# Spreading POOL's additions of y over four slots in an attention and GELU kernel

## The chip, the cores and the metric

The kernel runs on one core of one Trainium2 chip. The metric is the device time of one execution in microseconds; the kernel before takes 1471.4 us (median of three runs, 1471.25 to 1472.25). The core's engines work side by side, each through its own instructions in order: TensorE (PE in the profile; PEld is its loading of weights) multiplies matrices into PSUM, VectorE is DVE, ScalarE is ACT, GpSimd is POOL, and SyncE (SP) issues DMAs here.

## The reference

```python
# attention: q, k, v are (8, 8, 576, 64), float32
scores = scale * np.matmul(q, k.transpose(0, 1, 3, 2))
kth = np.partition(scores, -top_k, axis=-1)[..., -top_k:-top_k + 1]   # top_k = 32
scores = np.where(scores >= kth, scores, -1000000000.0)
attn = np.exp(scores - np.max(scores, axis=-1, keepdims=True))
attn = attn / (np.sum(attn, axis=-1, keepdims=True) + 1e-09)
x = np.matmul(attn, v)            # then (B, H, S, D) -> (4608, 512)
# mlp: w_in is (512, 2048), w_out is (2048, 512)
h = x @ w_in
g = 0.5 * h * (1.0 + erf(h * inv_sqrt2))
out = g @ w_out
```

Each row of scores keeps only its 32 largest entries; then a softmax, the product with v, and a two-layer network with an exact GELU.

## The kernel before

**Slots.** The attention is cut into 144 items, each a tile of 128 query rows for a pair of heads. The main loop runs over slots n = 0 to 147, and every slot issues one step of several items at once: scores of items n+2 and n+3 (PE, then ACT), the search for the 32nd largest score of item n (DVE, `top_k`), selection and softmax of item n-1 (ACT, lines 538 and 550), transposition of item n-2, the product with v of item n-3 (PE, `attend`, tile o, line 736 or 747). All engines take the instructions in the order in which the loop writes them; there is no planner, and an engine runs ahead of the others as far as its data and buffers allow.

**The top-k.** DVE halves the work by keeping, of every two scores, the larger in one list (`larger`, line 443) and the smaller in another. POOL makes the second list: `sum_up` (line 468) adds the two as integers, `smaller` (line 476) subtracts the larger. DVE then alternates maxima of eight (line 504) with replacements (line 507).

**POOL's slot.** Once the top-k of item n has ended, POOL computes the threshold (lines 518 and 519), multiplies item n-1 by the inverse of its sum (`normalise`, line 573), and sums the lists of item n+2 (line 468). Behind that stands what the change touches, `run_small`. The next slot brings `smaller` (476) and the small addition to the softmax's sum (line 531, `add_small`), for whose result DVE waits with its reciprocal (line 525) at the end of its top-k. ACT's selection of the next slot waits for the threshold.

**Transposing by DMA.** From the middle of the run on, half of the items go through HBM: DVE transposes blocks (line 599), SP writes the tile (`write_p`, line 609, tensor turned) and reads it back in the next slot (`read_p`, line 619, tile pt), which PE then uses as weights of o.

**The network.** As soon as the rows of x for a block of tokens are there, its products go into the slots in pieces: even slots take the first layer (tile h_ps, line 805), odd ones the second layer. A block has 256 tokens, or 128 at the end of the sequences. For 256 tokens the second layer is computed with seven products in place of eight (tiles seven and y_ps, lines 959 and 961). For that POOL forms four sums of each group of gelus (`sums`, lines 842 to 845), right behind the gelus, and adds the products up afterwards.

**The additions.** These go to a list, `small`, as pairs of a size and a function. In each of the second to fourth odd slots of a block one addition of the seventh product is put at its head (line 982; ACT has copied that product to tile p in line 980). The last slot of a block adds seven more: lines 1010 to 1014, then `lower` (line 1021) and `upper` (line 1025). The last two also register the store of 128 finished rows, which SP issues one slot later (line 876). `run_small(room)` first runs the sums that are due, each for 4 of its room, and then takes from the list while room is left:

```python
        while summing:
            sums(summing.pop(0))
            room -= 4
        while small and room > 0:
            n, f = small.pop(0)
            f()
            room -= n
```

A block of 128 tokens needs no sums and ends with one entry of size 2 (lines 936 and 937). Tiles y, part and y7 have two buffers each. `few[0]` is true from slot 13 on, when PSUM is shared more sparingly. Past slot 144 the pieces that are left run one after the other, and `run_small(9)` is called from elsewhere.

Of the kernel before, what the change touches and what calls it, by code (L numbers as in the profile page):

```python
# [14 lines left out]
def kernel(  # L15
# [261 lines left out]
    few = [False]  # L277
# [552 lines left out]
    def sums(u):  # L830

        g = g_of[u].rearrange("p x (f n) -> p x f n", f=2)
        a11, a21, a12, a22 = (g[:, :, f, h * P : (h + 1) * P] for f in range(2) for h in range(2))
        if u == NU - 2:
            t = work.tile([P, 2 * S], f32, tag="s", bufs=7, name="sum_s")
            t = t[:, 0 : 6 * P].rearrange("p (x k n) -> p x k n", x=2, k=3)
            add = nc.vector.tensor_tensor
        else:
            t = work.tile([P, 2, 3, P], f32, tag="sum", bufs=1, name="sum")
            add = nc.gpsimd.tensor_tensor  # L840
        s1, s2, s4 = (t[:, :, x] for x in range(3))
        add(s1, a21, a22, op=ALU.add)
        add(s2, s1, a11, op=ALU.subtract)
        add(a21, a11, a21, op=ALU.subtract)
        add(s4, a12, s2, op=ALU.subtract)
        sums_of[u] = t

    def weight_sums(j):

        e, o = w_out_sb[:, 2 * j], w_out_sb[:, 2 * j + 1]  # L850
        t2, t3, t4 = (w_sum[:, j, x] for x in range(3))
        nc.gpsimd.tensor_tensor(t3, o[:, B2], e[:, B2], op=ALU.subtract)
        nc.gpsimd.tensor_tensor(e[:, B2], e[:, B2], e[:, B1], op=ALU.subtract)
        nc.gpsimd.tensor_tensor(t2, o[:, B2], e[:, B2], op=ALU.subtract)
        nc.gpsimd.tensor_tensor(t4, t2, o[:, B1], op=ALU.subtract)
        summed.add(j)

    summing, summed = [], set()
# [107 lines left out]
    seven, small = [None], []  # L966
# [121 lines left out]
    def run_small(room):  # L1088
# [8 lines that stand above are left out]
# [93 lines left out]
    for n in range(ahead):  # L1190
# [149 lines left out]
        sum_up(n + 2)  # L1340
        if n in sums_in:
            weight_sums(sums_in[n])
        run_small(6)

        if n > 0 and not waits(unit_in(n + 1)):
            weights_size(unit_in(n + 1))
# [52 lines left out]
```

## Time and profile before

| | |
|---|---|
| median of the runs | 1471.4 us (1471.25 to 1472.25) |
| profiled execution | 1471.37 us |
| its span, first to last instruction | 1469.6 us |
| PE, DVE, POOL, ACT busy | 99%, 89%, 77%, 73% |
| POOL, one addition of 128 x 256 | 0.73 us |
| POOL, normalise (line 573) | 2.12 us |
| POOL, lines 468 and 476 | 1.43 and 1.41 us |

The profile is of one execution. In rows of the timeline stand start, duration, engine, line, operation, the tile written and the tiles read, and in brackets how long the engine had been idle and what it waited for. A row of waits reads "engine, tile and line that waited, what released it: us in total, times, longest". In the chain a row has the start, the time and the engine with its tile and line. Ends of matmuls are modelled: each is shown longer than the distance to the next.

### The profile page before, as it was taken

Reading aid. Unit: us, or ns where it says so; the run is one execution under the profiler, and the core shown is the slowest. Engines: PE = TensorE matmul, PEld = TensorE weight load, DVE = VectorE, ACT = ScalarE, POOL = GpSimd, SP = SyncE. Lnnn points to the kernel's source line nnn. Section 1 sums busy time; section 2 is a strip of 40 time slices with the busy share of each in tenths; the row PEclk is TensorE's granted clock in tenths of the full one; section 3 lists DMA queues with packets and bytes.
Section 4 is the critical chain, followed back from the end, with each engine's and each line's share of the span. In section 5 each row is a group of like instructions: output and inputs, shape, how many; then the busy total and the mean of one; then the engine's idle time right before and its main releaser. Section 6 shows DMA issues by size and latency. Waiting matters only on the chain. (4 is left out here: it accounts for less than half of the span.)

```text
span 1469.6 us, 26630 instructions
## 1 busy us (share of the span) xinstructions
PE 1450.9 (99%) x8720; PEld 1135.9 (77%) x8720; DVE 1312.0 (89%) x3328; ACT 1069.3 (73%) x1905; POOL 1138.1 (77%) x1290
## 2 busy tenths in 40 slices
PE   8999999999999999999999999999999999999999
PEld 6776677877777777887777778787777777787887
DVE  7999899999999899999999999999989989999701
ACT  7999977777777786767777777776777767687620
POOL 6877667878798879877798978887888887987632
PEclk9999999999999999999999999999999999999999
DMA  7524210045435246345534345444543423633200
GB/s 196 147 87 127 82 48 1 24 92 109 79 76 96 56 84 134 65 102 107 106 75 83 71 71 119 87 92 95 104 96 75 89 48 81 128 66 74 62 15 15
DMA packets 527050, 123.51 MB, mean 84 GB/s; under 512 B 452256, under 2 KB 518464, under 8 KB 526912
## 3 DMA queue, kind: packets, MB, share of 16 engines
q1 hardware_dynamic: 525648, 121.39, 38.7%
q8 instruction: 69, 1.13, 0.3%
q14 instruction: 69, 0.57, 0.1%
q10 hardware_dynamic: 1200, 0.39, 0.1%
q0 software_dynamic: 64, 0.03, 0.0%
HBM read 78.70 MB, written 43.06 MB: 83 GB/s over the span
## 5 line engine op out<-in xcount | busy, mean ns | idle before, releaser
L805 PE MATMUL h_ps<-xT,w_in_sb 128*128 128x256 f32 (+1 forms) x2560 | 534.1, 361 | 0.0
L805 PEld LDWEIGHTS h_ps<-xT,w_in_sb 128*128 128x128 f32 x2560 | 437.5, 190 | 73.3 <-issue 12.9
L504 DVE MAX8 top<-lists 128x8 f32<-128x576 f32 (+1 forms) x792 | 475.3, 639 | 0.0
L507 DVE MATCH_REPLACE8 lists<-top,lists 128x288 f32<-128x288 f32 (+1 forms) x528 | 307.4, 587 | 0.0
L538 ACT ACTIVATE s<-s,stat 128x576 f32<-128x576 f32 x288 | 217.6, 778 | 100.9 <-POOL stat L518 100.9
L573 POOL TENSOR_TENSOR s<-s,stat 128x1152 f32<-128x1152 f32 x135 | 285.9, 2118 | 0.3 <-DVE stat L525 0.3
L550 ACT ACTIVATE s<-s,stat 128x576 f32<-128x576 f32 x288 | 223.7, 780 | 7.3
L468 POOL TENSOR_TENSOR lists<-s 128x576 int32<-128x576 int32 x133 | 189.8, 1427 | 0.0
L476 POOL TENSOR_TENSOR lists<-lists 128x576 int32<-128x576 int32 x132 | 186.1, 1410 | 4.0
L531 POOL TENSOR_SCALAR stat<-stat 128x2 f32<-128x2 f32 x144 | 31.4, 218 | 166.6 <-ACT s L550 160.3
L736 PE MATMUL o<-pt,raw_v 128*64 128x256 f32 x1280 | 152.9, 384 | 3.2 <-DMA pt<-turned 2.0
L416 ACT ACTIVATE s<-s_ps 128x1024 f32<-128x1024 f32 x127 | 124.9, 1030 | 42.1 <-PE s_ps L408 42.0
L736 PEld LDWEIGHTS o<-pt,raw_v 128*64 128x64 f32 x1280 | 87.5, 136 | 87.5 <-issue 42.2
L961 PE MATMUL y_ps<-w_out_sb,sum 128*128 128x256 f32 x472 | 140.4, 379 | 0.0
L408 PE MATMUL s_ps<-kt,qm 64*128 64x512 f32 x512 | 129.6, 619 | 0.8 <-ACT s L414 0.8
L821 ACT ACTIVATE g<-h_ps 128x512 f32<-128x512 f32 x144 | 78.2, 595 | 71.1 <-PE h_ps L805 70.5
L961 PE MATMUL y_ps<-w_out_sb,g 128*128 128x256 f32 x480 | 114.2, 380 | 0.0
L507 DVE MATCH_REPLACE8 lists<-first,lists 128x288 f32<-128x288 f32 x264 | 114.1, 437 | 0.0
L443 DVE TENSOR_TENSOR lists<-s 128x576 f32<-128x576 f32 x133 | 108.6, 817 | 4.3 <-ACT s L381 2.2
L504 DVE MAX8 first<-lists 128x8 f32<-128x288 f32 x268 | 106.3, 435 | 0.0
L680 ACT COPY pt<-tp 128x1024 f32<-128x1024 f32 x76 | 77.6, 1021 | 37.4 <-PE tp L665 37.3
L961 PEld LDWEIGHTS y_ps<-w_out_sb,g 128*128 128x128 f32 x480 | 91.0, 190 | 12.4
(162 smaller groups left out, 2406.9 us busy)
## 6 DMA issues: line engine op xcount, KB each, us to landing
turned<-s SPq DMA_DIRECT2D x228, 144.0 KB, 3.6
pt<-turned SPq DMA_DIRECT2D x228, 144.0 KB, 3.1
raw_v<-in_v_dram SPq DMA_DIRECT2D x64, 128.0 KB, 2.6
raw_q<-in_q_dram SPq DMA_DIRECT2D x112, 72.0 KB, 2.4
raw_k<-in_k_dram SPq DMA_DIRECT2D x112, 72.0 KB, 2.4
out_dram<-y SPq DMA_DIRECT2D x30, 256.0 KB, 2.2
w_out_sb<-in_moe_w_in_dram SPq DMA_DIRECT2D x14, 511.8 KB, 4.9
w_out_sb<-in_moe_w_out_dram SPq DMA_DIRECT2D x10, 511.8 KB, 4.1
```

The source lines that it names most:

```text
L408: nc.tensor.matmul(s_ps[:, e], lhsT=q_t[rows, :], rhs=kt[rows, main_keys(pair)], start=True, stop=True)
L416: nc.scalar.activation(spread(s, S + TL, SM), s_ps, func=AF.Copy, scale=scale)
L468: nc.gpsimd.tensor_tensor(t[:, :, 1].bitcast(i32), a.bitcast(i32), b.bitcast(i32), op=ALU.add)
L476: nc.gpsimd.tensor_tensor(into_of(i)[:, :, 1].bitcast(i32), both, top, op=ALU.subtract)
L504: nc.vector.max(x[:, e], src[:, e])
L507: nc.vector.match_replace(dst[:, e], x[:, e], src[:, e], LOWEST)
L538: nc.scalar.activation(s, s, func=AF.Prelu, bias=st["neg"][:, e : e + 1], scale=1.0, alpha=STEEP)
L550: nc.scalar.activation(s, s, func=AF.Exp, bias=st["bias"][:, e : e + 1], scale=1.0, accum_out=st["den"][:, e : e + 1],)
L573: nc.gpsimd.tensor_tensor(s, s, wide, op=ALU.mult)
L736: nc.tensor.matmul(o[e * D : (e + 1) * D, 0:n], lhsT=vt[:, j, e, :], rhs=pt[:, e * NJ + j if j < NM else NM, :], start=(j == 0), stop=(j = ...
L805: nc.tensor.matmul(h_tile(u)[:, i, :], lhsT=w_in_sb[:, ko, f * P : (f + 1) * P], rhs=xT[:, ko, c0 : c0 + n], start=(ko == 0), stop=(ko == ...
L961: nc.tensor.matmul(acc[names][:, k], lhsT=lhsT, rhs=rhs, start=(j == 0 and k == 0), stop=(j == FT // 2 - 1 and k == 1),)
```

## The change

The room given to `run_small` at the end of a slot becomes dependent on what the slot holds. From slot 13 on, a slot with sums gets 5 in place of 6, so one entry of the list follows the sums. A slot without sums gets the length of the list less three, at least three.

```diff
@@ -1340,7 +1340,7 @@
         sum_up(n + 2)
         if n in sums_in:
             weight_sums(sums_in[n])
-        run_small(6)
+        run_small(6 if not few[0] else 5 if summing else max(3, len(small) - 3))
 
         if n > 0 and not waits(unit_in(n + 1)):
             weights_size(unit_in(n + 1))
```

## The prediction

> **What bounds the kernel now.** I read the page's busy rows first, then the chain for the rate of TensorE, then what each engine waited for, then the stretch of one batch of additions in order of time.
>
> ```profile
> PE 1450.9 (99%) x8720; PEld 1135.9 (77%) x8720; DVE 1312.0 (89%) x3328; ACT 1069.3 (73%) x1905; POOL 1138.1 (77%) x1290
> ```
> ```profile
> 1293.69 1.92 PE s_ps L408 x8
> 1408.13 6.91 PE h_ps L805 x32
> ```
> ```profile
> L805 PEld LDWEIGHTS h_ps<-xT,w_in_sb 128*128 128x128 f32 x2560 | 437.5, 190 | 73.3 <-issue 12.9 <-ACT s L538 12.3 <-ACT g L821 0.5
> ```
>
> TensorE is busy for 99% of the span. A busy PE need not be at its peak, so the rate decides: 32 matmuls took 6.91 us, 216 ns each, and the load of one weight tile takes 190 of these. Back to back there is nothing between them to win. A gain must therefore come out of moments when PE stood still. Behind the start-up and ahead of the tail (130 to 1360 us) these are all the waits of PE, and below them those of DVE:
>
> ```profile
> PE o L736 <- DMA pt<-turned: 2.0, 2, 1.2
> PE tp_t L373 <- ACT p L980: 1.2, 3, 0.4
> PE o L747 <- ACT p L980: 0.8, 3, 0.3
> PE o L736 <- issue: 0.4, 1, 0.4
> ```
> ```profile
> DVE stat L525 <- POOL stat L531: 65.1, 65, 2.9
> DVE lists L443 <- ACT s L381: 2.2, 4, 0.7
> ```
>
> So PE lost some 4.4 us in 1230, while DVE stood 65 us waiting for POOL's L531. DVE's lateness is absorbed by buffers, nearly always. The question is whether the few waits of PE come from the slots with six additions. These are the six that are not of o L747, and the matmuls ahead of the last:
>
> ```profile
> 424.81 0.49 PE L373 MATMUL tp_t<-kt,qm 128*128 128x128 f32 x2 [0.41 <-ACT p L980]
> 584.95 0.62 PE L736 MATMUL o<-pt,raw_v 128*64 128x256 f32 x3 [0.37 <-issue]
> 770.26 0.49 PE L373 MATMUL tp_t<-kt,qm 128*128 128x128 f32 x2 [0.42 <-ACT p L980]
> 931.23 0.65 PE L736 MATMUL o<-pt,raw_v 128*64 128x256 f32 x4 [1.23 <-DMA pt<-turned]
> 1116.25 0.49 PE L373 MATMUL tp_t<-kt,qm 128*128 128x128 f32 x2 [0.40 <-ACT p L980]
> 1274.01 1.99 PE L408 MATMUL s_ps<-kt,qm 64*128 64x512 f32 x8
> 1276.73 0.62 PE L736 MATMUL o<-pt,raw_v 128*64 128x256 f32 x3 [0.73 <-DMA pt<-turned]
> ```
>
> By the code's count of slots, six additions stand together in slots 40, 48, 56, 76, 84, 92, 112, 120 and 128; the tp_t waits are in slots 43, 79 and 115, those of o in 60, 96 and 132, each three or four slots behind one. 584.95, 931.23 and 1276.73 are one ring of two batches apart (346.28 and 345.50), so I count the first, whose releaser the row calls issue, with the other two.
>
> **The change, part by part.** Call m the slot in which the last products of 256 tokens end. They leave eight additions (L982, L1010 to L1014, L1021, L1025). In nine of thirteen places the next gelus are summed in slots m and m+2. There the old rule does sums + 2, then 6, sums, nothing. The new one does sums + 1; then 7 are left and max(3, 7 - 3) = 4 run; then sums + 1; then 2. In the other four places (the next block has 128 tokens, no sums in m) 6 + 2 becomes 5 + 3. At the end of the program nothing differs, since run_small has another caller there. No instruction is added or removed. One place of the nine, POOL in order of time:
>
> ```profile
> 743.71 0.73 POOL L1010 TENSOR_TENSOR y<-y 128x256 f32<-128x256 f32 x1
> 744.39 1.41 POOL L476 TENSOR_TENSOR lists<-lists 128x576 int32<-128x576 int32 x1
> 750.42 0.72 POOL L1011 TENSOR_TENSOR y<-y,y 128x256 f32<-128x256 f32 x1
> 752.60 0.74 POOL L1014 TENSOR_TENSOR y<-y,y 128x256 f32<-128x256 f32 x1
> 753.28 0.74 POOL L1021 TENSOR_TENSOR y<-y,y 128x256 f32<-128x256 f32 x1
> 754.66 1.42 POOL L476 TENSOR_TENSOR lists<-lists 128x576 int32<-128x576 int32 x1
> 756.16 0.22 POOL L531 TENSOR_SCALAR stat<-stat 128x2 f32<-128x2 f32 x1
> 765.05 0.22 POOL L531 TENSOR_SCALAR stat<-stat 128x2 f32<-128x2 f32 x1
> 765.85 0.22 POOL L518 TENSOR_SCALAR stat<-top 128x2 f32<-128x2 f32 x1 [0.58 <-DVE stat L525]
> 770.20 1.40 POOL L476 TENSOR_TENSOR lists<-lists 128x576 int32<-128x576 int32 x1
> 773.23 0.22 POOL L531 TENSOR_SCALAR stat<-stat 128x2 f32<-128x2 f32 x1 [1.63 <-ACT s L550]
> ```
> ```profile
> 756.41 0.17 DVE L525 RECIPROCAL stat<-stat 128x2 f32<-128x2 f32 x1 [2.18 <-POOL stat L531]
> 756.49 0.76 DVE L443 TENSOR_TENSOR lists<-s 128x576 f32<-128x576 f32 x1
> ```
>
> Slot m: L1010 goes, and L476 and L531 come 744.39 - 743.71 = 0.68 us sooner. Slot m+1: L1014, L1021 and L1025 go (752.60 to 754.66, 2.06 us) and L1010 comes in (0.68), which saves 1.38 more. L531 falls from 756.16 to 754.10, and DVE, ready since 756.41 - 2.18 = 754.23 and that too up to 0.68 sooner, goes on 2.06 us earlier. Slot m+2: L1014 costs POOL 0.68, so its L531 comes 2.06 - 0.68 = 1.38 sooner; the threshold L518 waited there for DVE (0.58) and so comes between 1.38 and 2.06 sooner. ScalarE's selection hangs on that threshold, its gelus and the copy of p (L980) on the selection, and tp_t on that copy: 1.38 us covers a wait of 0.42. Slot m+3: two additions cost 754.66 - 753.28 = 1.38 us, between L468 and L476, and lie in POOL's idle time ahead of L531, 1.63 here. What hides them is that L531 waits for the softmax (L550) anyway; without that cover they cost DVE 1.38 us at each place. The smallest idle of that slot among the nine, and that of the last:
>
> ```profile
> 427.78 0.22 POOL L531 TENSOR_SCALAR stat<-stat 128x2 f32<-128x2 f32 x1 [1.61 <-ACT s L550]
> 1275.06 0.22 POOL L531 TENSOR_SCALAR stat<-stat 128x2 f32<-128x2 f32 x1 [1.97 <-ACT s L550]
> ```
>
> So I take nothing for them, with 12.4 us of DVE time (nine times 1.38) as the far end.
>
> The stores move too. L1021 and L1025 register them, and SP issues them in the slot behind: m+4 in place of m+2, the parity is kept. On SP this is what stands there in the third place of each ring:
>
> ```profile
> 1261.06 2.58 SPq L619 DMA_DIRECT2D pt<-turned  x4
> 1263.73 1.02 SPq L876 DMA_DIRECT2D out_dram<-y  x2
> 1264.85 4.00 SPq L609 DMA_DIRECT2D turned<-s  x4
> 1271.57 2.54 SPq L619 DMA_DIRECT2D pt<-turned  x4
> 1280.67 3.35 SPq L609 DMA_DIRECT2D turned<-s  x4
> ```
> ```profile
> 1261.80 1.36 DVE L599 STREAM_TRANSPOSE s<-s 128x1152 f32<-128x1152 f32 x1
> ```
>
> The data of the write at 1264.85 was there at 1263.16 (1261.80 + 1.36), and SP had been at the stores since 1263.73. Without them the write starts at about 1263.74, 1.1 us sooner, and so do the read behind it and PE's o, late by 0.73. In the new place the stores fall between 1274.11 and 1280.67, where SP has 6.5 us with nothing to issue: cost 0. What could be late next are the buffers: y, part and y7 have two each, and their next user in the nine places is ScalarE at slot m+8, behind the store of m+4; in the four others the additions end in m+1 as before.
>
> Sum: the waits of pt give 2.0 + 0.4, but of the 1.23 only the 1.1, so 2.3; those of tp_t 1.2. The idle time shown begins at the modelled end of a matmul; s_ps really hands on after 1.92 us and not 1.99 (0.07 three times). For tp_t the modelled 379 ns against 216 add 0.16 three times. Together 2.3 + 1.2 + 0.2 + 0.5 = 4.2 us. The three of o L747 (0.8) I leave in:
>
> ```profile
> 1263.83 0.27 ACT L757 COPY xT<-o 128x128 f32<-128x128 f32 x1 [2.19 <-PE o L747]
> ```
>
> ScalarE itself waits there for PE, so POOL is not their cause. The profiled execution took 1471.37 us (span 1469.6, 1.8 around it), the median of the runs is 1471.4: the forecast is 1471.4 - 4.2 = 1467.2. Whatever stays off PE's path comes to nothing, since the matmuls keep their 216 ns.
>
> **The rivals.** *DVE loses it again.* DVE's L443 reads two halves of s. Mostly it takes 0.76, but where it began late, beside POOL's normalisation, it took 2.61:
>
> ```profile
> 1339.36 2.61 DVE L443 TENSOR_TENSOR lists<-s 128x576 f32<-128x576 f32 x1 [0.46 <-ACT s L381]
> ```
>
> A DVE that is 2 us ahead meets s unfinished more often, and each meeting costs 2.61 - 0.76 = 1.85 of the 2.06. The tp_t waits would stay, and the store's share come: 1471.4 - 2.5 = 1468.9, not told from no change. Against it: only four waits on L381 in all now. The Trainium skill, SBUF — State Buffer, section SBUF: two separate sides, says that GpSimd and a VectorE instruction with two SBUF inputs take a shared port as an exclusive lock, the loser blocked for the whole instruction. By that rule this meeting is no accident; the 2.61 agrees with it.
>
> *The reads are not SP's.* If the waits for pt hang on how fast the DMAs land, only tp_t's 1.7 comes: 1469.7. For it speaks that the four writes took 4.00 us at 1264.85 and 3.35 at 1280.67, though the stores just ahead may be why.
>
> *Slower: the cover in slot m+3 is gone.* ScalarE's softmax ends sooner than POOL's two additions; it decides as soon as the 1.61 falls under 1.38. Then L531, DVE and the next threshold are late in a slot that had no such load, and each of nine places gains a tp_t wait of 0.58 while the old ones stay: 1471.4 + 5.2 = 1476.6. Against it: both sides of that idle time start from the same threshold, so shifting it leaves the 0.23 us of margin.
>
> *PE was not the bound.* Then DVE's 2.06 at nine places comes in full: 1471.4 - 18.5 = 1452.9. The Trainium skill, Perfetto Trace Analysis, section Identifying the Most-Contended Engine, says that matmul busy time misleads and that the share of weight loads is to be read. By that rule PE has 23% free here (77%), which would speak for this rival. The rows speak against it: 190 of 216 ns is 88% where nothing stands still.
>
> **How the numbers follow.** About 0.2%, 2.9 us, is what a measurement of this kernel tells from no change. Forecast (1465.0 to 1468.4): 0.60. DVE loses it again 0.13, reads not SP's 0.12: these two lie within 0.2%. Slower 0.11. PE not the bound 0.04. Faster: 0.60 less 0.02 for its upper edge, and 0.04, is 0.62; same 0.27; slower 0.11. The range takes in the forecast's own, whose low end has the L747 waits (0.8 and 0.5 of pipelining) and a little more gone, and both small rivals up to no change: 1465.0 to 1471.6; outside are the slower case and the large gain, 0.15.
>
> **What would show it.** POOL's timeline has 4, 1 and 2 additions in m+1, m+2, m+3. DVE's wait for L531 falls from 65 us by up to 18; L531's idle in m+3 falls from 1.6 to about 0.2. The waits of PE for pt and of tp_t for p are gone, and the stores stand behind a read with nothing on their heels. The forecast is wrong if PE's waits reappear behind m+3, if L443 takes over 2 us in new places, or if POOL's later L476 lets DVE wait in the middle of a top-k.

## The result, and the profile after

The changed kernel takes 1467.4 us in the median of nine runs (1467.1 to 1467.9), the kernel before beside it on the same chip 1471.6 (1470.9 to 1473.6): a ratio of 0.9971, with a 95% interval of 0.9961 to 0.9981. The forecast was 1467.2 us, within 1465.0 to 1471.6. The profiled execution took 1467.42 us, 3.95 less than the one of before, with a span of 1465.7.

The row of busy times of the changed kernel, which answers to the first row shown in the prediction:

```profile
PE 1449.4 (99%) x8720; PEld 1134.9 (77%) x8720; DVE 1313.4 (90%) x3328; ACT 1070.1 (73%) x1905; POOL 1137.9 (78%) x1290
```

The instructions are as many as before on every engine, and PE is still busy for 99%. The difference has to lie in the moments when PE stood still. All its waits between 130 and 1360 us in the changed kernel, then those of DVE (us in total, times, longest):

```profile
PE o L747 <- ACT p L980: 0.8, 3, 0.3
PE tp_t L373 <- ACT p L980: 0.5, 2, 0.3
```
```profile
DVE stat L525 <- POOL stat L531: 58.7, 70, 3.4
DVE lists L443 <- ACT s L381: 3.1, 5, 0.7
```

PE's waits for pt (2.4 us with the one put down to issue) are gone, and those of tp_t fell from 1.2 to 0.5. The total went from 4.4 to 1.3 us. That tp_t waits for a copy of another product comes from the code: from slot 13 on, tp_t (here the scores of the last keys, line 373), seven and o take turns in one PSUM buffer (`bank`, tag z). A tp_t behind seven can start only when ScalarE has copied that product out (L980, or L977 for the first of a block).

The place that the prediction showed, in the changed kernel, POOL in order of time:

```profile
742.65 1.42 POOL L476 TENSOR_TENSOR lists<-lists 128x576 int32<-128x576 int32 x1
...
748.69 0.73 POOL L1010 TENSOR_TENSOR y<-y 128x256 f32<-128x256 f32 x1
749.49 0.73 POOL L1011 TENSOR_TENSOR y<-y,y 128x256 f32<-128x256 f32 x1
...
751.56 1.41 POOL L476 TENSOR_TENSOR lists<-lists 128x576 int32<-128x576 int32 x1
...
760.47 0.74 POOL L1014 TENSOR_TENSOR y<-y,y 128x256 f32<-128x256 f32 x1
...
762.66 0.22 POOL L531 TENSOR_SCALAR stat<-stat 128x2 f32<-128x2 f32 x1
762.95 0.22 POOL L518 TENSOR_SCALAR stat<-top 128x2 f32<-128x2 f32 x1
...
767.88 0.73 POOL L1025 TENSOR_TENSOR y<-y,part 128x256 f32<-128x256 f32 x1
...
770.34 0.22 POOL L531 TENSOR_SCALAR stat<-stat 128x2 f32<-128x2 f32 x1 [0.36 <-ACT s L550]
```

The rows left out are marked by dots. Four additions (L1010 to L1013) stand in slot m+1, one (L1014) in m+2, two (L1021, L1025) in m+3. To see what that moved, the two kernels need a common clock. DVE's reciprocal ahead of this place, untouched by it, was at 735.75 before and at 734.67 after, so the changed kernel came into the place 1.08 us ahead. DVE in the kernel before, and then in the changed one:

```profile
735.75 0.14 DVE L525 RECIPROCAL stat<-stat 128x2 f32<-128x2 f32 x1
```
```profile
734.67 0.14 DVE L525 RECIPROCAL stat<-stat 128x2 f32<-128x2 f32 x1
...
753.31 0.17 DVE L525 RECIPROCAL stat<-stat 128x2 f32<-128x2 f32 x1 [0.81 <-POOL stat L531]
```

From there on, each step against the rows of the prediction, less 1.08: L476 behind slot m 0.66 us sooner (744.39 to 742.65), DVE's reciprocal behind slot m+1 2.02 sooner (756.41 to 753.31), L531 behind m+2 1.31 sooner (765.05 to 762.66), the threshold L518 there 1.82 sooner (765.85 to 762.95), L531 behind m+3 1.81 sooner (773.23 to 770.34). The idle time ahead of this last one fell from 1.63 to 0.36.

Where the 3.95 us arose is seen from the start of the same matmul in both traces: both kernels issue the same 8720 matmuls in the same order. This is by how much the changed kernel gained on the kernel before around each place, in us, worked out from the two traces:

```
at (us, before)   gained                 the matmul
 425, 770, 1116   +0.67  +0.69  +0.66    tp_t L373
 585, 931, 1277   +0.26  +1.30  +0.80    o L736, reading pt
 579, 924, 1270   +0.17  +0.15  +0.16    small steps up to tp_t L651
 598, 944, 1290   -0.08  -0.52  -0.53    tp_t L373
1388              +0.15                  the tail
```

The tp_t matmuls give 2.02, those of pt 2.36, the small steps 0.48 and the end 0.15; 1.13 go back. The rest of 0.1 is in hundredths. What goes back is new waits of tp_t some 13 us behind each pt place. PE in the changed kernel, at a place where it had no wait before:

```profile
941.42 0.49 PE L373 MATMUL tp_t<-kt,qm 128*128 128x128 f32 x2 [0.26 <-ACT p L980]
```

SP at the third place of the ring, in the changed kernel (the rows that answer to those of the prediction), and below it PE's matmuls, the last of which read that pt:

```profile
1256.42 3.09 SPq L619 DMA_DIRECT2D pt<-turned  x4
1259.62 3.46 SPq L609 DMA_DIRECT2D turned<-s  x4
1265.78 3.56 SPq L619 DMA_DIRECT2D pt<-turned  x4
1269.38 1.07 SPq L876 DMA_DIRECT2D out_dram<-y  x2
1277.13 3.36 SPq L609 DMA_DIRECT2D turned<-s  x4
```
```profile
1270.47 1.99 PE L408 MATMUL s_ps<-kt,qm 64*128 64x512 f32 x8
1272.39 2.38 PE L736 MATMUL o<-pt,raw_v 128*64 128x256 f32 x20
```

The write follows the read at once, and the stores stand behind the next read with 6.68 us free after them (1270.45 to 1277.13). PE goes from s_ps to o without a gap.

### The profile page after: what moved, and what is told of

Same layout as the page of the kernel before. It is cut to its first block, busy times and chain, and to the rows that moved or that the text cites. A ratio compares the mean times of both kernels' runs of the same rounds, so it can differ in the third digit from the quotient of the medians.

```text
span 1465.7 us, 26622 instructions
## 1 busy us (share of the span) xinstructions
PE 1449.4 (99%) x8720; PEld 1134.9 (77%) x8720; DVE 1313.4 (90%) x3328; ACT 1070.1 (73%) x1905; POOL 1137.9 (78%) x1290
## 3 DMA queue, kind: packets, MB, share of 16 engines
q8 instruction: 69, 1.13, 0.3%
## 5 line engine op out<-in xcount | busy, mean ns | idle before, releaser
L573 POOL TENSOR_TENSOR s<-s,stat 128x1152 f32<-128x1152 f32 x135 | 286.4, 2121 | 0.3 <-DVE stat L525 0.3
L550 ACT ACTIVATE s<-s,stat 128x576 f32<-128x576 f32 x288 | 224.1, 781 | 7.5 <-issue 0.4
L476 POOL TENSOR_TENSOR lists<-lists 128x576 int32<-128x576 int32 x132 | 186.2, 1411 | 3.3
L531 POOL TENSOR_SCALAR stat<-stat 128x2 f32<-128x2 f32 x144 | 31.4, 218 | 167.2 <-ACT s L550 155.8
L736 PE MATMUL o<-pt,raw_v 128*64 128x256 f32 x1280 | 152.9, 384 | 0.9 <-ACT pt L670 0.4
L736 PEld LDWEIGHTS o<-pt,raw_v 128*64 128x64 f32 x1280 | 86.9, 136 | 85.7 <-issue 42.6
L821 ACT ACTIVATE g<-h_ps 128x512 f32<-128x512 f32 x144 | 78.2, 594 | 75.7 <-PE h_ps L805 75.2
L443 DVE TENSOR_TENSOR lists<-s 128x576 f32<-128x576 f32 x133 | 109.9, 827 | 5.1 <-ACT s L381 3.1
L680 ACT COPY pt<-tp 128x1024 f32<-128x1024 f32 x76 | 77.6, 1020 | 39.9 <-PE tp L665 39.7
```

The lines of the kernel that those rows point to most:

```text
L476: nc.gpsimd.tensor_tensor(into_of(i)[:, :, 1].bitcast(i32), both, top, op=ALU.subtract)
L550: nc.scalar.activation(s, s, func=AF.Exp, bias=st["bias"][:, e : e + 1], scale=1.0, accum_out=st["den"][:, e : e + 1],)
L573: nc.gpsimd.tensor_tensor(s, s, wide, op=ALU.mult)
L736: nc.tensor.matmul(o[e * D : (e + 1) * D, 0:n], lhsT=vt[:, j, e, :], rhs=pt[:, e * NJ + j if j < NM else NM, :], start=(j == 0), stop=(j = ...
```

## The experiments

The change does two things at once: it moves stores by two slots, and it spreads additions. The table gives each kernel by the additions that it has in slots m, m+1, m+2 and m+3 of the nine places. "Late" stores stand where the changed kernel has them, "early" ones where the kernel before has them. Kernel before in the four calls: 1471.6, 1471.3, 1471.5 and 1471.7 us.

| kernel | additions | stores | us | ratio to before (95%) |
|---|---|---|---|---|
| before | 2, 6, 0, 0 | early | 1471.6 | 1 |
| changed | 1, 4, 1, 2 | late | 1467.4 | 0.9971 (0.9961 to 0.9981) |
| stores_late | 2, 6, 0, 0 | late | 1470.4 | 0.9991 (0.9982 to 0.9999) |
| dummy_stores | 1, 4, 1, 2 | late, and dummies early | 1469.4 | 0.9989 (0.9980 to 0.9998) |
| eight_in_one | 0, 8, 0, 0 | early | 1474.4 | 1.0017 (1.0008 to 1.0026) |
| four_four | 4, 4, 0, 0 | early | 1480.4 | 1.0058 (1.0045 to 1.0070) |
| one_in_m | 1, 7, 0, 0 | late | 1471.5 | 0.9998 (0.9989 to 1.0007) |
| two_in_m | 2, 4, 0, 2 | late | 1467.6 | 0.9973 (0.9962 to 0.9983) |
| four_last | 1, 3, 0, 4 | late | 1467.6 | 0.9969 (0.9956 to 0.9981) |
| six_later | 1, 0, 0, 7 | late | 1472.7 | 1.0007 (0.9998 to 1.0016) |
| no_seven | 1, 0, 0, 0 | late | 1467.3 | 0.9967 (0.9955 to 0.9980) |
| p_first | 1, 4, 1, 2 | late | 1493.1 | 1.0144 (1.0131 to 1.0158) |

### The stores alone: stores_late

The additions stay as before. The stores go through one more list and are issued two slots later.

```diff
-                stores.append(lambda to=to, part=part: nc.sync.dma_start(out=to, in_=part))
+                (held_back[1] if late else stores).append(
+                    lambda to=to, part=part: nc.sync.dma_start(out=to, in_=part)
+                )
...
         older[:] = stores
-        stores.clear()
+        stores[:] = held_back.pop(0)
+        held_back.append([])
...
-            store(tok + P, y1)
+            store(tok + P, y1, tok % RING != 256)
```

> POOL's additions stand as in the kernel before (2, 6, 0, 0 in slots m to m+3); only the stores of the nine places go out two slots later, at the place on SP that the changed kernel gives them. Theory (two causes: the stores ahead of a write on SP make PE wait for pt, the additions on POOL make it wait for p): the waits of o L736 for pt (2.4 us before) go, the three tp_t waits (0.40 to 0.42 each) stay; 1471.6 - 2.5 = about 1469.1 us. Rival (the additions on POOL are behind all of it, the write waits for DVE): the pt waits stay and the time is that of before, 1471.6.

1470.4 us against 1471.3. PE's waits in this kernel, between 130 and 1360 us:

```profile
PE tp_t L373 <- ACT p L983: 2.4, 6, 0.4
PE o L747 <- ACT p L983: 0.8, 3, 0.3
```

Not one wait for pt is left, so the place of the stores made those waits. But the tp_t waits went from three to six. By starts of the same matmuls, the three old ones stay as they were, 2.35 us are won at the three o L736 (0.32, 1.30 and 0.73), and 1.68 go back at the tp_t behind them (0.32, 0.72 and 0.64). PE is now earlier at a matmul that hangs on ScalarE's copy, and that copy has not moved.

### The stores' old place loaded again: dummy_stores

The changed kernel, with two dummy DMAs of 256 KB each at the place that the stores have left.

```diff
+    spare_out = [dram.tile([P, DM], f32, tag=f"spare{x}", bufs=1, name="spare") for x in range(2)]
...
+        if few[0] and len(small) == 7 and not summing:
+            stores.extend(
+                lambda t=t: nc.sync.dma_start(out=t, in_=w_out_sb[:, 0, :]) for t in spare_out
+            )
         run_small(6 if not few[0] else 5 if summing else max(3, len(small) - 3))
```

> The changed kernel, and in the nine places two more DMAs of 256 KB from a weight tile to a spare buffer in HBM, issued by SP where the kernel before had its two stores. Nothing else moves. Theory (two DMAs ahead of a write are enough to make PE wait for pt): the pt waits come back at about 584, 930 and 1275 us, 2.4 us of PE in all, and the tp_t waits behind them (0.25, 0.42, 0.43) go, as in the kernel before; 1467.4 + 1.4 = 1468.8 us. Rival (the place on SP was not the cause): 1467.4 us.

1469.4 us (1467.9 to 1474.8, a wider spread than the others'). PE's waits, and SP and PE at the third place:

```profile
PE o L736 <- DMA pt<-turned: 2.5, 3, 1.3
```
```profile
1261.21 1.08 SPq L1346 DMA_DIRECT2D spare<-w_out_sb  x2
1262.40 3.80 SPq L609 DMA_DIRECT2D turned<-s  x4
```
```profile
1274.26 2.38 PE L736 MATMUL o<-pt,raw_v 128*64 128x256 f32 x20 [1.33 <-DMA pt<-turned]
```

The waits for pt return, three of them and 2.5 us, though POOL's additions are spread as in the changed kernel. Two DMAs at that place on SP's queue make them, also when no result of POOL is in them. The write starts right behind their issue (1262.29 to 1262.40), as it did behind the stores in the kernel before, so that 1.1 us of its lateness are SP's issuing. Whether their bytes slow the write as well stays open, since the dummies carry as many as the stores. And the tp_t waits behind the pt places are gone from the list: PE, 0.3 to 1.3 us later there, finds the copy done. So 1.5 us of the profiled time come back (1468.9 against 1467.4) and not 2.5.

### Moving additions within the first two slots: eight_in_one, four_four and one_in_m

If only DVE's release behind slot m+1 counted, it would not matter how the eight additions are shared between m and m+1, and taking them out of m would even be free. eight_in_one puts all into m+1 (on the kernel before):

```diff
-        run_small(6)
+        eight = few[0] and len(small) == 8
+        run_small(6 if not eight else 4 if summing else 8 if n % 2 == 0 else 6)
```

> In the nine places nothing is added in slot m and all eight additions in slot m+1 (0, 8, 0, 0 in place of 2, 6, 0, 0); stores as before. Theory (what counts is the sum of additions that POOL has done by the end of m+1, eight in both): DVE waits less in m (0.92 us gone) and as much more in m+1 (about 3.1 in place of 2.18), L531 of m+1 comes at the same time, PE's waits and the time stay as before, 1471.6 us. Rival (the size of one batch counts): DVE and the next threshold are 1.4 us later at nine places, each with a longer tp_t or pt wait; 1474 to 1484 us.

1474.4 us, 3.1 slower. PE's waits, and DVE and PE at one place:

```profile
PE tp_t L373 <- ACT p L980: 3.2, 4, 1.0
PE o L736 <- DMA pt<-turned: 1.4, 2, 1.2
PE tp_t L651 <- POOL s L573: 1.0, 3, 0.4
PE seven L959 <- POOL g L844: 0.6, 3, 0.2
```
```profile
758.01 0.17 DVE L525 RECIPROCAL stat<-stat 128x2 f32<-128x2 f32 x1 [3.66 <-POOL stat L531]
```
```profile
771.86 0.49 PE L373 MATMUL tp_t<-kt,qm 128*128 128x128 f32 x2 [1.02 <-ACT p L980]
```

DVE's wait behind m+1 grew from 2.18 to 3.66, and tp_t's, which hangs on the threshold behind it, from 0.42 to 1.02. Besides, PE now waits for POOL itself, for its normalisation (L573) and its sums (L844), which the list of the kernel before doesn't have. What was taken out of m did not make up for it.

four_four moves two of the six the other way, into m, behind the gelus' sums (on the kernel before):

```diff
-        run_small(6)
+        run_small(8 if few[0] and summing and len(small) == 8 else 6)
```

> Nine places: 4, 4, 0, 0 additions in slots m to m+3 (before 2, 6, 0, 0; the run with 0, 8, 0, 0 was 3.1 us slower than before); stores as before. Theory (the lateness at the end of m+1 counts; POOL never waits for DVE in m, so eight additions cost the same however they are cut): 1471.5 us, the three tp_t waits of 0.57 stay, DVE waits 1.4 us more in m and as much less in m+1. Rival (the largest batch in one slot counts: 8 gave 1474.4, 6 gives 1471.5, so 4 gives less): about 1469 us, with tp_t waits shorter.

1480.4 us, 8.9 slower, though the slot with six had become one with four. The largest of PE's waits, and the chain behind slot m:

```profile
PE tp_t L373 <- ACT y L977: 6.3, 6, 1.1
```
```profile
751.05 0.17 DVE L525 RECIPROCAL stat<-stat 128x2 f32<-128x2 f32 x1 [2.42 <-POOL stat L531]
```
```profile
751.35 1.44 ACT L538 ACTIVATE s<-s,stat 128x576 f32<-128x576 f32 x2 [4.36 <-POOL stat L518]
...
755.07 0.38 ACT L977 COPY y<-seven 128x256 f32<-128x256 f32 x1
```
```profile
755.51 0.49 PE L373 MATMUL tp_t<-kt,qm 128*128 128x128 f32 x2 [1.06 <-ACT y L977]
```

The rows left out are the load of ScalarE's table and the gelus (both L821). The idea that only the release behind m+1 counts falls here. Behind slot m stands a threshold, and on it ScalarE's selection, its gelus, the copy of the next block's first seventh product (L977) and PE's tp_t: the same chain as behind m+2, two slots earlier. In the kernel before no tp_t waits for L977. Two more additions in m cost that room at once.

one_in_m has one addition in m and seven in m+1, with the stores late (on stores_late), to see whether slot m's 0.68 us is worth anything by itself:

```diff
-        run_small(6)
+        eight = few[0] and len(small) == 8 and summing
+        run_small(5 if eight else 7 if len(small) == 7 else 6)
```

> Nine places: 1, 7, 0, 0 additions in slots m to m+3; stores at the changed kernel's place on SP. Theory (DVE waits 0.92 us for L531 in m, so 0.68 less there is won in full and lost again in m+1, where L531 comes at the same time as with 2, 6, 0, 0): 1470.4 us as with the stores moved alone; 0, 8, 0, 0 was slower because only 0.92 of its 1.37 could be won in m. Rival (every addition more in m+1 costs): 1471.5 us or more.

1471.5 us. That is 1.1 above stores_late by the medians of two calls, and 0.9 in the two traces between 130 and 1360 us; the intervals of the two ratios overlap. The waits of tp_t are six again, 3.0 us in all:

```profile
PE tp_t L373 <- ACT p L983: 3.0, 6, 0.6
```

An addition moved from m to m+1 costs, though the sum of both slots is unchanged: DVE's release behind m+1 comes some 0.14 us later than in stores_late, and the old three waits of tp_t grow by 0.12 to 0.15 each. Nothing in PE's waits shows the 0.68 saved in m.

### Lightening m+1 alone: two_in_m

Two additions stay in m, two go from m+1 to m+3 (on the changed kernel).

```diff
+        eight = few[0] and len(small) == 8 and summing
+        run_small(6 if not few[0] or eight else (4 if len(small) == 2 else 5) if summing else max({6: 4}.get(len(small), 0), 3, len(small) - 3))
```

> Nine places: 2, 4, 0, 2 additions in slots m to m+3; stores as in the changed kernel. Against the run with the stores moved alone (2, 6, 0, 0; 1470.4 us) two additions go from m+1 to m+3, against the changed kernel (1, 4, 1, 2) one stays in m. Theory (the lightening of m+1, 1.38 us, is enough to take the three tp_t waits of 0.57 away, slot m's 0.68 is not needed): 1467.5 us. Rival (the slot with the sums is where an addition costs most, as 4, 4, 0, 0 with 1480.4 us suggests): some of the gain is missing, 1468.5 to 1470 us.

1467.6 us, the same as the changed kernel. Its waits of PE beside those of o L747, which stay:

```profile
PE o L736 <- DMA pt<-turned: 0.9, 1, 0.9
PE tp_t L373 <- ACT p L980: 0.5, 2, 0.3
```

One wait for pt is there, at 1273.6. In that read one of SP's four issues lasts 1.99 us where the others last 0.6; why was not followed up. It makes this one execution 0.5 us slower than the changed kernel's (1467.94), and hardly moves the median of seven. The tp_t waits at 425, 770 and 1116 are gone as in the changed kernel. So lightening slot m is no part of the gain that these runs can tell, and neither is the one addition behind the sums of m+2. What counts, beside the late stores, is that slot m+1 has four additions and not six, with no more than the old two in m.

### The cover in slot m+3: four_last and six_later

The slower rival was that the additions in m+3 outlast the softmax (L550) which hides them, with a margin of 0.23 us. four_last puts four there, 2.87 us (766.05 to 768.92 below) where the smallest idle time before was 1.61:

```diff
-        run_small(6 if not few[0] else 5 if summing else max(3, len(small) - 3))
+        nine = {8: 5, 7: 3, 4: 4}.get(len(small), 3)
+        run_small(6 if not few[0] else (4 if len(small) == 4 else 5) if summing else nine)
```

> Nine places: 1, 3, 0, 4 additions in slots m to m+3, in place of the changed kernel's 1, 4, 1, 2; stores as in the changed kernel. Theory (in m+3 the additions lie in POOL's idle time ahead of L531, 1.61 us without them): four cost 2.75 us, 1.1 more than that, so L531's idle in m+3 is 0.1 where it was 0.36, DVE waits about 1 us more there; in exchange m+1 and m+2 are 0.7 and 1.4 us lighter. If PE's waits follow DVE's lateness, tp_t waits come back behind m+3: 1468.5 us. Rival (DVE has room by then, the cover is of no account): 1467.4 us as the changed kernel, or less.

1467.6 us, as fast as the changed kernel. POOL at one place, and PE's wait beside those of o L747:

```profile
766.05 0.73 POOL L1013 TENSOR_TENSOR y<-y 128x256 f32<-128x256 f32 x1
...
768.92 1.42 POOL L476 TENSOR_TENSOR lists<-lists 128x576 int32<-128x576 int32 x1
770.42 0.22 POOL L531 TENSOR_SCALAR stat<-stat 128x2 f32<-128x2 f32 x1
```
```profile
PE tp_t L373 <- ACT p L980: 0.8, 3, 0.3
```

L531 now waits for nothing, so the cover is used up, and PE loses nothing by it. The deciding point of that rival, an idle time under 1.38, was wrong.

six_later takes all additions out of m+1 and m+2 and puts them into m+3. The expectation counts six of them, but they are seven (L1010 to L1014, L1021 and L1025), since slot m keeps only the one of L982.

```diff
+    NO_ADD = [x % 36 for x in (40, 48, 56)]
...
+        nine = {8: 5, 7: 0 if n % 36 in NO_ADD else 7}.get(len(small), 3)
+        run_small(6 if not few[0] else (4 if len(small) == 7 else 5) if summing else nine)
```

> Nine places: 1, 0, 0, 6 additions in slots m to m+3; stores as in the changed kernel. The six are again in one slot, but two slots later, in front of POOL's idle time ahead of L531 (2.0 us in slots like 78 without additions, over 5 in slots like 86, 3.5 in slots like 94). Theory (the place of the six counts, not that they stand together): 4.1 us of additions exceed the idle time by about 2 us in three places and 0.7 in three, so some tp_t wait comes back there, and the time is between 1467.5 and 1469. Rival (spreading counts): the time of the kernel with the stores moved alone, 1470.4 us.

1472.7 us, 5.3 above the changed kernel. The largest of PE's waits, and ScalarE and PE at one place:

```profile
PE tp_t L373 <- ACT p L980: 5.1, 3, 1.8
```
```profile
941.24 1.44 ACT L538 ACTIVATE s<-s,stat 128x576 f32<-128x576 f32 x2 [5.00 <-POOL stat L518]
```
```profile
945.40 0.49 PE L373 MATMUL tp_t<-kt,qm 128*128 128x128 f32 x2 [1.70 <-ACT p L980]
```

Only three of the nine places bring such a wait, about 1.7 us each, and these are the same three where the changed kernel gives a little back (598, 944 and 1290 in the table above). By starts of the same matmuls, 0.26 to 0.29 more go at each of three s_ps (467, 811 and 1155), whose cause was not followed up. So the slower rival is a real mechanism with the price put at the wrong point: it bites beyond four additions, by seven, and at three places and not at nine.

### What these additions cost at all: no_seven

The changed kernel without the seven last additions of a block, up to slot 144; that part of y is not computed.

```diff
+        def pool(*x, op):
+            if n_slot[0] > N:
+                nc.gpsimd.tensor_tensor(*x, op=op)
...
+        few[0], n_slot[0] = n > START + 2, n
```

> The changed kernel with the seven last additions of each block of 256 tokens (L1010 to L1014, L1021, L1025) left out up to slot 144, so the rows stored there lack these sums; the stores stand where the changed kernel has them, and L982 stays. Theory: the three o L747 waits (0.43 us of PE each by the distance of matmuls) are not POOL's doing and stay; of the changed kernel's remaining waits in the middle those for p in tp_t (0.25, 0.42, 0.43) go: 1467.4 - 1.1 = 1466.3 us. Rival (POOL is still the limit in the changed kernel): the L747 waits go too, 1465 us or less.

1467.3 us, with an interval that holds that of the changed kernel nearly whole. Its waits of PE:

```profile
PE o L747 <- ACT p L980: 0.8, 3, 0.3
PE tp_t L373 <- ACT p L980: 0.8, 3, 0.3
```

The three waits of o L747 stay, as the prediction had it. But three tp_t waits stay too (597, 941 and 1286), where I had expected none; they are 0.42 to 0.44 each with the 0.16 that the modelled end of the matmul ahead hides. They are the ones that the changed kernel has, where that at 597 is too short for the list: the additions do not make them. Without these seven the time is the same, so there is nothing left to win by placing these seven better.

### The copy that tp_t waits for: p_first

PE's remaining waits of tp_t hang on ScalarE's copy of p, which stands behind the gelus. On the changed kernel, the gelus are issued one piece later, so that the copy goes first.

```diff
-        if few[0] and n % 2:
-            run_gelus()
         tr = transposes(n - 2)
...
         mlp(1)
+        if few[0] and n % 2:
+            run_gelus()
```

> The changed kernel with the gelus of odd slots issued one piece later, so that ScalarE copies the seventh product (L980) ahead of the table load and the two gelus. Theory (the waits of tp_t and of o L747 that are left, six or so of 0.25 to 0.43 us, come because L980 stands behind the gelus on ScalarE, 3.4 us): they go, and unless the gelus' lateness makes the sums late for PE's next products, 1467.4 - 2.3 = 1465.1 us. Rival (ScalarE then waits for PE's seventh product, 0.9 us more ahead of the gelus, POOL's sums come later and DVE behind them): slower than the changed kernel, 1468 to 1472 us.

1493.1 us, 25.7 above the changed kernel, far beyond any of the cases. The two largest of PE's waits:

```profile
PE s_ps L408 <- ACT pt L680: 11.4, 19, 0.7
PE s_ps L423 <- ACT pt L680: 2.7, 6, 0.6
```

PE's scores (s_ps) now wait for ScalarE's copy of the transposed tiles (L680), 14.1 us that are in no other kernel here. So the copy of p can't go ahead of the gelus in this way; where the rest of the 25.7 us lies was not followed up.

## Why the prediction was right, and where its working was not

**PE is the bound, and the gain is in its waits.** This held. PE stays at 99%, its waits fell by 3.1 us in the rows of waits and the start-to-start comparison puts 3.95 on single matmuls. The rival by which PE is not the bound would have given 18.5 us.

**Additions 1, 4, 1, 2 and the shifts.** These held to 0.07 us at the first three slots: 0.66 (0.68 forecast), 2.02 (2.06), 1.31 (1.38). The threshold came 1.82 sooner, within 1.38 to 2.06. The idle time of L531 in m+3 fell to 0.36 at the place shown, near the forecast 0.2.

**The waits of tp_t.** They were forecast at 1.7 and measured at 2.02 at the three places. The 0.16 added for each is right for the first matmul of a row: it gained 0.57, 0.59 and 0.56 where the rows had 0.41, 0.42 and 0.40. The second matmul, merged into the same row, gained another 0.10 each time, and the sum left that out.

**The waits for pt and the stores.** They were forecast at 2.5 (2.3 and 0.2) and measured at 2.36, in part by luck: the wait of 1.23 went whole (1.30, where the sum took 1.1 and 0.07), and the first place gave 0.26 of the 0.44 (0.37 and 0.07) counted for it. The cause stands on two runs: stores_late lost the waits by moving only the stores, dummy_stores regained them by putting something else in their place. The three waits belonged together, the one put down to issue too. The rival that the reads are not SP's falls as to the time. Its observation, that the write took 4.00 us there, is not put down to the stores: it took 3.46 without them, but another write of the changed kernel, at 588.35 and with no store ahead, takes 4.21. The new place of the stores cost nothing that the traces show.

**What the sum left out.** It left out two terms. The small steps between L373 and L651 gave 0.48. And the tp_t behind each pt place gave back 1.13, since PE, now ahead, arrives there before ScalarE's copy. The prediction had named waits of PE behind m+3 as a sign that it is wrong; they came, but no_seven has them too, so the additions are not their cause. That a wait removed at one place returns in part at the next was missing from the sum. These terms offset each other in part, so a sum of 4.2 against 3.95 in the profiles (4.17 in the medians) looks better than its parts: the tp_t and pt terms measured 4.38.

**DVE's gain.** The wait for L531 fell by 6.4 us in place of up to 18. It was no part of the sum, but one limit was missed: most of the time comes back two slots later as other waits of DVE for the same line (70 in place of 65). Added up from the traces over the nine places, DVE's waits fell from 21.9 to 6.3 us in m and m+1, and rose from 8.3 to 18.0 in m+2 and m+3. A DVE that is earlier waits in m+2 for a POOL that is busy right up to L531 and has L1014 to do besides, and in m+3, at six of the places, for an L531 that stands idle itself, in five of them waiting for the softmax (L550). The other sign named for a wrong forecast came as well, a long L443 in a new place:

```profile
341.72 2.48 DVE L443 TENSOR_TENSOR lists<-s 128x576 f32<-128x576 f32 x1 [0.59 <-ACT s L381]
```

There are five L443 of over 2 us in place of four, and each of them begins while POOL's normalisation (L573) runs, as the prediction read it for the one of 2.61. None of PE's waits hangs on them, and the rival's two effects did not come: the tp_t waits at its places went, and the time is 1.5 us below its 1468.9. The sign was chosen too sharp. The third sign, a DVE that waits in the middle of a top-k, did not come: lines 525 and 443 are the only ones in its list of waits.

**What each part was worth.** The prediction charged 0.68 us in m and 0.68 in m+2 to the same account as the 1.38 in m+1. two_in_m shows that, beside the late stores, the lighter m+1 does it. The costs in m+3 were put at zero for the right row, but with a margin of 0.23 us that four_last shows to be no edge at all: behind L531 there is more slack in DVE and ScalarE, down to PE's copy.

**Stores and additions are not separate terms.** The stores alone gave 0.9 us (1471.3 to 1470.4), and 2.0 on top of the additions (1469.4 to 1467.4). The additions gave 2.1 with the old place loaded (1471.5 to 1469.4), and 3.0 on top of the late stores (1470.4 to 1467.4). The 1469.4 is the median of runs that lie between 1467.9 and 1474.8, so the two figures that use it are rough. How the sum splits depends on the order in which it is taken.

## What to carry to other kernels

When the bound engine is busy for 99%, list its few waits with their places and ask of each which queue or slot ends it last; then expect that a removed wait gives part of its time to the next one that hangs on an unmoved chain. The same seven or eight short instructions cost between nothing and 13 us here (1467.3 to 1480.4, the stores' place included) by the slot in which they stand, so find the slots behind which a release feeds the bound engine, and put work into the others. Of an in-order DMA queue, look at what stands directly ahead of a transfer whose reader is on the path.

## What the runs showed of the hardware

POOL's additions of 128 x 256 last 0.73 us each. Back to back, they start 0.68 to 0.70 us apart where the next one is independent of the one ahead, and 0.79 to 0.82 where it reads what that one has just written or overwrites what that one reads. This holds for every such pair of L1010 to L1025 in the traces of before, after, eight_in_one and six_later; that the dependence is the reason is read from the code. In the changed kernel L1010 to L1011 are 0.80 apart (748.69 to 749.49), where L1011 reads what L1010 writes. In six_later, where all seven stand together, POOL's rows show both:

```profile
926.77 0.72 POOL L1013 TENSOR_TENSOR y<-y 128x256 f32<-128x256 f32 x1
927.57 0.73 POOL L1014 TENSOR_TENSOR y<-y,y 128x256 f32<-128x256 f32 x1
928.26 0.72 POOL L1021 TENSOR_TENSOR y<-y,y 128x256 f32<-128x256 f32 x1
```

L1014 overwrites a half tile that L1013 reads (0.80); L1021 writes another half, which L1014 does not touch (0.69). Where a chain of additions is cut thus changes its cost by some 0.11 us for each dependent joint.
